# A spectral layer fused with a rational MLP on one core: padded input, later tables, ten first-stage tasks at the end of batch 0, and an offset copied into PSUM instead of added by a matmul

## The chip, the cores and the metric

The kernel runs on one core of a Trainium2 chip. The metric is device microseconds (us) of that core, median of three runs. TensorE (PE) multiplies, VectorE (DVE), ScalarE (ACT) and GpSimd (POOL) do elementwise work, SyncE (SP) issues most DMAs. [...]

## What is computed

```python
X = np.fft.rfft(x, axis=1)                       # x: 4 batches, 3008 rows, 256 columns
Yr = Xr @ w_r - Xi @ w_i + b_r
Yi = Xr @ w_i + Xi @ w_r + b_i
Y = soft_threshold(Yr, 0.01) + 1j * soft_threshold(Yi, 0.01)
x = np.fft.irfft(Y, n=3008, axis=1)              # then, row by row:
h = x @ w_in                                     # 256 -> 2048
g = (a0 + a1*h + a2*h**2 + a3*h**3) / (1 + |b0|*|h| + |b1|*h**2 + 1e-6)
out = g @ w_out                                  # 2048 -> 256
```

`w_in` and `w_out` come as 64-bit floats; the chip turns them into pairs of 32-bit numbers.

## The kernel before

A transform of length 3008 = 64 x 47 is done in two stages. For each batch, 16 first-stage tasks (`f1_task`, L158) multiply a tile of `x` by the table `f1` and put the result in HBM (`s1`). Twelve second-stage tasks (`f2_task`, L209) read it back in another order. Twelve mixing tasks (`m_task`, L237) multiply by `w_r` and `w_i`, 24 matmuls each, add the offsets `b_r`, `b_i` and threshold. Twelve `i1_task`s (L264) start the inverse transform and store to HBM (`s2`); `i2_task` (L307) ends it, two per block of five columns. The MLP then runs in 208 units (`h` L350, the rational function on ACT, DVE, POOL and an adding DMA `v<-s`, `acc` L440).

**Batch 0** runs alone, ahead of the MLP. Its first stage is a loop over 16 tasks; its tiles `a` go to HBM by SP (L187). PE then runs `warm(38)`, matmuls on zeros (L509), while the tiles come back as `b_all`. The loop at L612 makes 15 rounds, p = 0 to 14. In round p PE does `f2_task(p)`, then the two halves of `m_task(p-2)`, then `i1_task(p-3)`. ACT, DVE and POOL do what belongs to them (`x` L221, L224, L230; `yt` L258, L261; `zt` L145/L147), and between these the conversion of the weights, called by `convert(n)`, which makes n steps of `from_f64`: ACT's `e` and `r` (L482, L483), DVE's L485 and L487, DVE's L489 followed by ACT's copy `win` or `wsp` (L494), POOL's L496. The tuples `HC` and `HM` say how many steps stand ahead of `yt` and behind it in each round. An m task opens its PSUM bank `pm` with one matmul, `selr` by `bias` (L245), which writes the offsets; the 24 others (L252) add to them. `prepare_small` (L526) makes `selr` and `bias` on DVE behind the last first-stage tasks.

**Batch 0's end.** After the rounds, six more first-stage tasks of batch 1 run (two have run in round 13, eight in all, `FILL = 8`), with two conversion steps behind each; then the first two `i2_task`s and the first product `h` (unit 0).

**The main part** walks through the units i; in each, the letters of `order` say when PE products, ACT's two halves and the transform tasks of the next batch are issued. Batch 1's other first-stage tasks go into its first units. There the offsets are put into the bank by an ACT copy of the tile `offset` (L242, from unit 3 on).

Of the kernel before, what the change touches and what calls it, by code (L numbers as in the profile page):

```python
# [9 lines left out]
F32 = mybir.dt.float32  # L10
# [4 lines left out]
ALU = mybir.AluOpType  # L15
# [21 lines left out]
def dft_tables():  # L37
# [14 lines left out]
    for g in range(NG):  # L52
# [24 lines left out]
    i2p = i2b.reshape(96, TJ)  # L77
    sel = np.zeros((4, 130))
    sel[0:2, 0:64] = 1.0
    sel[2:4, 64:128] = 1.0  # L80
    sel[0::2, 128] = 1.0
    sel[1::2, 129] = 1.0
    f = np.float32
# [11 lines left out]
def spectral_moe(ctx, tc, t, out):  # L95
# [37 lines left out]
    def load_x(b, c):  # L133
        if b == 1 and c in (2, 3):
            xt = pro3.tile([96, 4, D], F32, tag=f"x{c}", name="xin", bufs=1)
        elif b == 0 and c >= 2:
            xt = const.tile([128, 4, D], F32, tag=f"win{c}", name="xin")[:96]
# [19 lines left out]

    def f1_task(b, i):  # L158
        c, r = divmod(i, 2)
        if i == 0:  # L160
            s1[b] = dram.tile([NK, NG, 2, NJ, D], F32, tag="s1", name="s1")
        pt = bank(b, "f1" if r else "")
        nc.tensor.matmul(out=pt, lhsT=f1, rhs=xin[b, c][:, 2 * r:2 * r + 2, :].rearrange("p j d -> p (j d)"),  # L163
                         start=True, stop=True)
        yield
        if b == 0:
            if not r:
                a_t[0] = const.tile([128, 4, D], F32, tag=f"wsp{c}", name="a")[:96]
            at = a_t[0][:, 2 * r:2 * r + 2]
        else:  # L170
            if early:
                at = pro.tile([128, 2, D], F32, tag="a" if i < 6 else "wt", name="a", bufs=6 if i < 6 else 2)[:96]
            else:
                at = sm.tile([128, 2, D], F32, tag="a", name="a", bufs=3)[:96]
        copy(i % 2 if early else 0, at.rearrange("p j d -> p (j d)"), pt[:96])
        yield
        if r:
            del xin[b, c]
            ahead = 4 if b == 1 and c < 4 else 2
            if b and c + ahead < NJ // 4 and not (b == 1 and c in (2, 3)):  # L180
                if early:
                    hold.append(lambda: load_x(b, c + ahead))
                else:
                    load_x(b, c + ahead)
        if b == 0:
            if r:
                nc.sync.dma_start(out=s1[b].rearrange("k g c j d -> (k g c) j d")[:, 4 * c:4 * c + 4, :], in_=a_t[0])  # L187
# [46 lines left out]
    y_t = {}  # L234
    copied = []
# [28 lines left out]
    def i1_task(b, p):  # L264
# [186 lines left out]
    def drain(g):  # L451
        for _ in g:
            pass

    def fft_tasks(b):
        ts = [(0.87, 1, 1, f1_task(b, i), 0) for i in range(16)]
        ts += [(0.0, 0, 0, load_first(b), 0)] + [(0.0, 0, 0, iter(()), 0)]
# [40 lines left out]
    with tc.manual_schedule():  # L498
        nc.vector.memset(cb, 1.0)
        nc.scalar.activation(out=cb, in_=cb, func=ACTF.Abs_reciprocal_sqrt)  # L500
        nc.sync.dma_start(out=f1, in_=t["f1"])
        b_all = [pro3.tile([128, 6, D], F32, tag=f"b{z}", name="b_all", bufs=1) for z in range(4)]
        nc.vector.memset(offset[:, 0], 0.0)
        idle = offset[:, 0].bitcast(mybir.dt.bfloat16)

# [13 lines left out]
        def load_small():
            nc.sync.dma_start(out=sel, in_=t["sel"])  # L520
            for k, nm in enumerate(("b_r", "b_i")):
                nc.sync.dma_start(out=bsb[2 * k:2 * k + 2, :],
                                  in_=t[nm].rearrange("(o d) -> o d", o=1).to_broadcast([2, D]))
            nc.sync.dma_start(out=eye, in_=t["minus"])

        def prepare_small():  # L526
            nc.vector.memset(v32(selr), 0.0)
            nc.vector.memset(v32(bias), 0.0)
            nc.vector.tensor_copy(selr[:4], sel[:, 0:128])
            nc.scalar.activation(out=minus, in_=eye, func=ACTF.Copy)  # L530
            bhi = bias[:4, 0]
            nc.vector.tensor_copy(bhi, bsb)
            nc.vector.tensor_tensor(out=blo, in0=bsb, in1=v32(bhi), op=ALU.subtract)
            nc.vector.tensor_scalar(out=bsb, in0=v32(bhi), scalar1=sel[:, 128:129], scalar2=None, op0=ALU.mult)
            for k in range(2):
                nc.vector.scalar_tensor_tensor(out=bias[:4, k], in0=blo, scalar=sel[:, 129:130], in1=bsb, op0=ALU.mult, op1=ALU.add)

# [73 lines left out]
        first = fft_tasks(1)  # L611
        for p in range(np_ + 3):  # L612
            if p < np_:
                f2g = f2_task(0, p)
                next(f2g)
                next(f2g)
# [39 lines left out]
            if p == 8:  # L656
                root()
                for k, nm in enumerate(("b_r", "b_i")):
                    for z in range(2):
                        nc.sync.dma_start(out=offset[64 * k:64 * k + 64, z],  # L660
                                          in_=t[nm].rearrange("(o d) -> o d", o=1).to_broadcast([64, D]))
# [30 lines left out]
        for i in range(-1, nu + 4):  # L692
# [111 lines left out]
```

## Time and profile before

| | us |
|---|---|
| median of 3 runs | 1453.56 (1453.04 to 1459.46) |
| the profiled execution | 1454.01 |
| its span in the trace | 1452.2 |
| PE busy | 1421.4 (98%) |
| DVE busy | 1297.3 (89%) |
| ACT busy | 1135.9 (78%) |
| POOL busy | 668.6 (46%) |

The profile is of one execution. Its own time is 1.8 us above the span and 0.45 us above the median. Times in its views count from the span's start. Matmuls overlap on PE, so a matmul's row is longer than the step to the next one. [...]

### The profile page before, as it was taken

What the parts mean: (1) busy time and instruction counts of PE and PEld (TensorE: products, weight loads), DVE (VectorE), ACT (ScalarE), POOL (GpSimd) and SP (SyncE); (2) the same over time, 40 slices, a digit from 0 to 9 for tenths busy, and PEclk for the clock granted to TensorE, in tenths of its full rate; (3) what the DMA queues carried; (4) which work ended last, traced back from release to release, by engine and by line L of the source; (5) the groups of instructions that cost most, each with busy time, mean ns of one, the idle gap of its engine ahead of it and who ended that gap; (6) DMA issues with size and microseconds to landing.
All of it is one profiled execution on the core that took longest, in us unless ns stands there. A gap on an engine that the chain in (4) does not pass through costs nothing.

```text
span 1452.2 us, 20182 instructions
## 1 busy us (share of the span) xinstructions
PE 1421.4 (98%) x7437; PEld 1242.8 (86%) x7439; DVE 1297.3 (89%) x1303; ACT 1135.9 (78%) x1438; POOL 668.6 (46%) x446
## 2 busy tenths in 40 slices
PE   8989999999999999999999999999999999999996
PEld 3966999999878999999888899998988888888886
DVE  3776889999888998898889999999989999999998
ACT  2657778787787777778888788878778988889885
POOL 0433444444444444444445445454445555555553
PEclk9998999999999999999999999999999999999999
DMA  8956545446575554554586455555455555546443
GB/s 264 374 177 154 120 104 122 104 103 134 130 189 130 124 111 103 122 131 95 121 195 149 105 118 104 121 111 119 92 114 118 107 107 108 116 98 121 92 93 70
DMA packets 84437, 187.60 MB, mean 129 GB/s; under 512 B 8363, under 2 KB 42835, under 8 KB 84339
## 3 DMA queue, kind: packets, MB, share of 16 engines
q0 software_dynamic: 30976, 98.58, 38.0%
q1 hardware_dynamic: 52467, 86.16, 18.6%
q10 hardware_dynamic: 896, 1.57, 0.3%
q8 instruction: 59, 0.97, 0.3%
q14 instruction: 39, 0.32, 0.1%
HBM read 50.23 MB, written 37.49 MB: 60 GB/s over the span
## 4 chain that ended last, share of the span: by engine, by line
PE 75%; DVE 9%; issue 8%; DMA 4%; ACT 3%; SPq 0%; ACTq 0%; DVEq 0%; POOL 0%; POOLq 0%
PE h L350 29%; PE acc L440 28%; PE pft L252 7%; PE pi L316 4%; PE pft L163 3%; DVE t L397 3%; DMA v<-s 2%; PE pft L270 2%; DVE v L408 2%; PE pft L216 2%; DVE g L406 1%; DMA raw_win<-in_w_in 1%; DVE e L489 1%; DMA s<-a 1%; DVE t L398 1%
## 5 line engine op out<-in xcount | busy, mean ns | idle before, releaser
L440 PE MATMUL acc<-g,wsp 128*128 128x470 f32 (+1 forms) x2496 | 561.2, 373 | 6.0 <-DVE g L419 6.0
L413 POOL TENSOR_TENSOR t<-t,v 128x940 f32<-128x940 f32 (+1 forms) x206 | 477.3, 2317 | 121.4 <-DVE v L408 107.8
L440 PEld LDWEIGHTS acc<-g,wsp 128*128 128x128 f32 x2496 | 466.2, 189 | 67.7 <-DVE g L419 6.9
L383 POOL DMA_DIRECT2D v<-s x208 | 186.3, 896 | 571.9 <-issue 526.7
L350 PE MATMUL h<-xsh,win 128*128 128x470 f32 (+1 forms) x1664 | 440.7, 387 | 7.1 <-DVE t L398 5.3
L350 PEld LDWEIGHTS h<-xsh,win 128*128 128x128 f32 x1664 | 305.0, 191 | 59.1 <-issue 12.7
L381 ACT ACTIVATE v<-h 128x940 f32<-128x940 f32 (+1 forms) x208 | 196.2, 943 | 155.9 <-PE h L350 155.4
L406 DVE SCALAR_TENSOR_TENSOR g<-t,small,y 128x940 fp32r<-128x940 f32 (+1 forms) x208 | 255.2, 1227 | 61.2 <-ACT y L392 59.7
L397 DVE TENSOR_TENSOR t<-t,h 128x940 f32<-128x940 f32 (+1 forms) x208 | 231.4, 1113 | 38.2 <-ACT t L385 37.7
L398 DVE SCALAR_TENSOR_TENSOR t<-t,small,h 128x940 f32<-128x940 f32 (+1 forms) x208 | 245.2, 1179 | 7.4
L419 DVE SCALAR_TENSOR_TENSOR g<-t,small,y 128x940 fp32r<-128x940 f32 (+1 forms) x208 | 244.1, 1173 | 0.1
L350 PE MATMUL h<-xsl,win 128*128 128x470 f32 (+1 forms) x832 | 243.3, 374 | 0.0
L408 DVE SCALAR_TENSOR_TENSOR v<-v,g 128x940 f32<-128x940 f32 (+1 forms) x208 | 231.7, 1114 | 0.0
L390 ACT ACTIVATE y<-v 128x940 f32<-128x940 f32 (+1 forms) x208 | 205.6, 988 | 17.2 <-DMA v<-s 17.0
L385 ACT ACTIVATE t<-h,small 128x940 f32<-128x940 f32 (+1 forms) x208 | 215.7, 1037 | 0.0
L392 ACT ACTIVATE y<-y 128x940 f32<-128x940 f32 (+1 forms) x208 | 203.7, 979 | 2.3
L382 ACT ACTIVATE s<-h 128x940 f32<-128x940 f32 (+1 forms) x208 | 195.3, 939 | 0.0
L350 PEld LDWEIGHTS h<-xsl,win 128*128 128x128 f32 x832 | 156.2, 189 | 20.9
L252 PE MATMUL pft<-wrh,x 128*128 128x256 f32 x288 | 76.6, 288 | 1.1 <-ACT pft L147 1.1
L252 PE MATMUL pft<-wih,x 128*128 128x256 f32 x288 | 75.4, 283 | 0.4 <-DVE x L228 0.4
L316 PEld LDWEIGHTS pi<-small,ct 96*128 96x128 f32 x512 | 65.1, 192 | 5.5 <-ACT a L147 3.0
L316 PE MATMUL pi<-small,ct 96*128 96x94 f32 x512 | 64.3, 272 | 2.1 <-ACT a L147 2.1
(88 smaller groups left out, 1110.5 us busy)
## 6 DMA issues: line engine op xcount, KB each, us to landing
v<-s POOLq DMA_DIRECT2D x200, 470.0 KB, 4.6
xin<-in_x SPq DMA_DIRECT2D x32, 384.0 KB, 6.6
s<-zt SPq DMA_DIRECT2D x48, 256.0 KB, 2.7
out_t<-ob SPq DMA_DIRECT2D x50, 235.0 KB, 4.5
ct<-s SPq DMA_DIRECT2D x21, 480.0 KB, 5.2
bt<-s SPq DMA_DIRECT2D x36, 256.0 KB, 3.9
s<-a SPq DMA_DIRECT2D x40, 192.0 KB, 4.2
raw_win<-in_w_in SPq DMA_DIRECT2D x8, 512.0 KB, 10.3
```

Of the source, the lines that this page charges most:

```text
L252: nc.tensor.matmul(out=pt[:, k, :], lhsT=l, rhs=r, start=False, stop=n == len(ops) - 1, skip_group_check=True)
L350: nc.tensor.matmul(out=h[:, i, :w], lhsT=l, rhs=r, start=k == 0, stop=k == len(halves) // FU - 1)
L385: nc.scalar.activation(out=d["t"], in_=h, func=ACTF.Identity, scale=rate["a3"], bias=ca[:, 2:3])
L390: nc.scalar.activation(out=d["y"], in_=d["v"], func=ACTF.Square, bias=C0)
L392: nc.scalar.activation(out=d["y"], in_=d["y"], func=ACTF.Abs_reciprocal_sqrt)
L397: nc.vector.tensor_tensor(out=tt, in0=tt, in1=h, op=ALU.mult)
L398: nc.vector.scalar_tensor_tensor(out=tt, in0=tt, scalar=ca[:, 1:2], in1=h, op0=ALU.add, op1=ALU.mult)
L406: stt(out=hi, in0=tt, scalar=ca[:, 0:1], in1=y, op0=ALU.add, op1=ALU.mult)
L408: stt(out=v, in0=v, scalar=C0, in1=v32(hi), op0=ALU.add, op1=ALU.mult)
L413: nc.gpsimd.tensor_tensor(out=tt[:, :cut], in0=tt[:, :cut], in1=v[:, :cut], op=ALU.subtract)
L419: stt(out=lo, in0=tt, scalar=ca[:, 0:1], in1=y, op0=ALU.add, op1=ALU.mult)
L440: nc.tensor.matmul(out=acc[n][e][:, :w], lhsT=l, rhs=r, start=begun[n] == 1 and seen[e] == 1, stop=begun[n] == UB and seen[e] == 3 * FU)
```

## The change

Nine things are changed.

1. `x` is laid out as one block of 128 rows by 4 KB for each tile (96 rows of data, 32 of zeros), and tiles are loaded with 128 rows; tile 0 of batch 0 in two halves. `w_r` and `w_i` are laid out so that a row is contiguous.
2. The table `f1` is loaded by ACT's queue, `f2`, `w_r`, `w_i` behind all first-stage stores, `eye` behind `f2`. The last first-stage tile is stored in two halves.
3. `sel`, `bsb`, `selr`, `bias` and `prepare_small` are gone. The tile `offset` is loaded by four DMAs between the fourth and the fifth tile of `x`.
4. The matmul L245 is gone. `m_begin` copies `offset` into the bank by ACT. For batch 0 it is called at the head of rounds 2 to 13, ahead of `f2_task`.
5. `minus` is made in round 8 behind `root`.
6. All twelve copies `zt` of batch 0 are made by DVE (six by ACT before).
7. `warm(38)` becomes `warm(23)`, `warm(7)` becomes `warm(8)`.
8. `FILL` goes from 8 to 10, with one conversion step per task instead of two; `HM` is 6 instead of 4 in rounds 12 and 13. Tasks 12 and 13 of batch 1 run ahead of 8 to 11.
9. In units 0 to 3 `order` puts ACT's first-stage copies (`e`) ahead of the second half of the function (`Y`, `y`).

```diff
-WARM = 38
-FILL = 8
+WARM = 23
+FILL = 10
-HM = (0, 0, 3, 3, 3, 3, 3, 3, 3, 3, 3, 3, 4, 4)
+HM = (0, 0, 3, 3, 3, 3, 3, 3, 3, 3, 3, 3, 6, 6)
...
-            xt = sm.tile([96, 4, D], F32, tag="xin", name="xin")
-        nc.sync.dma_start(out=xt, in_=t["x"][b, :, 4 * c:4 * c + 4, :])
-        xin[b, c] = xt
+            xt = sm.tile([128, 4, D], F32, tag="xin", name="xin")
+        for r in (0, 2) if b + c == 0 else (0,):
+            w = 2 if b + c == 0 else 4
+            nc.sync.dma_start(out=xt[:, r:r + w], in_=t["x"][b, c, :, r:r + w, :])
+        xin[b, c] = xt[:96]
...
+    def m_begin(b):
+        m_t[b] = bank(b, "m").rearrange("p (k d) -> p k d", k=2)
+        copy(0, m_t[b], offset)
+
     def m_task(b, p, k):
-        if k == 0:
-            m_t[b] = bank(b, "m").rearrange("p (k d) -> p k d", k=2)
+        if k == 0 and b:
+            m_begin(b)
         pt = m_t[b]
         xs = x_t[b, p]
-        if k == 0 and copied:
-            copy(0, pt, offset)
-        elif k == 0:
-            nc.tensor.matmul(out=pt, lhsT=selr, rhs=bias, start=True, stop=False, skip_group_check=True)
...
-        copy(b == 0 and p % 2 == 0, zt.rearrange("p k d -> p (k d)"), pt.rearrange("p k d -> p (k d)"))
+        copy(b == 0, zt.rearrange("p k d -> p (k d)"), pt.rearrange("p k d -> p (k d)"))
...
-        load_small()
         for i in range(16):
-            drain(f1_task(0, i))
-            if i == 9:
-                load_f2(0, 4)
-                load_wt()
-            if i == 13:
-                prepare_small()
-            if i == 15:
-                prepare_mix()
+            drain(f1_task(0, i, i))
+        load_f2(0, 4)
+        load_wt()
+        prepare_mix()
...
         for p in range(np_ + 3):
+            if 2 <= p < np_ + 2:
+                m_begin(0)
             if p < np_:
                 f2g = f2_task(0, p)
...
         for _ in range(FILL - 2):
             drain(first.pop(0)[3])
-            convert(2)
+            convert(1)
...
-            order = "F1AasYehmy2" if storing(i) else "Fs1AaYehmy2"
+            order = "Fs1AaehmYy2" if i < 4 else "F1AasYehmy2" if storing(i) else "Fs1AaYehmy2"
```

**ACT in rounds 2 to 4.** First the program before, from the threshold `yt` of round 2 to the one of round 4 (a `yt` reads the bank `pm` that the round's m task has filled; `x` is ACT's half of the round's second-stage tile):

```order
L258 ACTIVATE yt_347<-pm_321 128x512
L482 ACTIVATE e_350<-raw_win1_221 128x512
L483 ACTIVATE r_351<-raw_win1_221 128x512
L494 ACTIVATE win0_355<-e_315 128x2x256
L221 ACTIVATE x_365<-pft_360 128x4x128
L482 ACTIVATE e_374<-raw_win2_275 128x512
L483 ACTIVATE r_375<-raw_win2_275 128x512
L258 ACTIVATE yt_404<-pm_378 128x512
L494 ACTIVATE win1_408<-e_350 128x2x256
L221 ACTIVATE x_425<-pft_420 128x4x128
```

The same stretch of the changed program, whose lines have other numbers (L252 is `yt`, L477 and L478 are `e` and `r`, L489 is `win`, L217 is `x`, L144 the copy of the offsets):

```order
L252 ACTIVATE yt_324<-pm_277 128x512
L477 ACTIVATE e_327<-raw_win1_213 128x512
L478 ACTIVATE r_328<-raw_win1_213 128x512
L489 ACTIVATE win0_332<-e_294 128x2x256
L144 ACTIVATE pm_337<-offset_73 128x512
L217 ACTIVATE x_344<-pft_339 128x4x128
L477 ACTIVATE e_353<-raw_win2_252 128x512
L478 ACTIVATE r_354<-raw_win2_252 128x512
L252 ACTIVATE yt_381<-pm_337 128x512
L489 ACTIVATE win1_385<-e_327 128x2x256
L144 ACTIVATE pm_397<-offset_73 128x512
L217 ACTIVATE x_404<-pft_399 128x4x128
```

The copy into `pm` stands behind the conversion's last step of the round before (`win`) and ahead of `x`. PE's first matmul of the m task that writes this `pm` waits for ACT.

**SP at the program's start.** Before (`s` is HBM behind the first stage, `a` its tiles, `f` the table `f2`):

```order
L501 DMA small<-in_f 96x128
L140 DMA xin<-in_x 96x1024 x8
L520 DMA sel<-in_sel 4x130
L522 DMA bsb<-in_b_r 2x256
L522 DMA bsb<-in_b_i 2x256
L524 DMA eye<-in_minus 128x128
L187 DMA s_131<-a 96x1024 x5
L579 DMA f_70<-in_f 128x512
L589 DMA wt<-in_w_r 128x2x256
L589 DMA wt<-in_w_i 128x2x256
L187 DMA s_131<-a 96x1024 x3
L576 DMA b_all<-s_131 128x2x256 x3
```

And in the changed program:

```order
L137 DMA xin<-in_x 128x512 x2
L137 DMA xin<-in_x 128x1024 x3
L509 DMA offset<-in_b_r 64x256 x2
L509 DMA offset<-in_b_i 64x256 x2
L137 DMA xin<-in_x 128x1024 x4
L183 DMA s_129<-a 96x1024 x7
L183 DMA s_129<-a 96x512 x2
L561 DMA f_70<-in_f 128x512
L571 DMA wt<-in_w_r 128x512
L571 DMA wt<-in_w_i 128x512
L558 DMA b_all<-s_129 128x2x256 x2
```

The eight stores now follow one another with no table between them, and four loads of `offset` stand between the tiles of `x`.

**ACT in unit 1.** Before (`v`, `s`, `t` are the first half of the function for unit 1, `y` the second half for unit 0, which reads `v` behind the adding DMA, `a` two copies of first-stage tiles):

```order
L381 ACTIVATE v_1161<-h_1113 128x940
L382 ACTIVATE s_1160<-h_1113 128x940
L385 ACTIVATE t_1162<-h_1113,small_69 128x940
L390 ACTIVATE y_1167<-v_1127 128x940
L147 ACTIVATE a_1169<-pft_1143 96x512
L147 ACTIVATE a_1171<-pft_1145 96x512
L392 ACTIVATE y_1167<-y_1167 128x940
```

And changed:

```order
L375 ACTIVATE v_1147<-h_1101 128x940
L376 ACTIVATE s_1146<-h_1101 128x940
L379 ACTIVATE t_1148<-h_1101,small_69 128x940
L144 ACTIVATE a_1153<-pft_1129 96x512
L144 ACTIVATE a_1155<-pft_1131 96x512
L384 ACTIVATE y_1157<-v_1115 128x940
L386 ACTIVATE y_1157<-y_1157 128x940
```

The two copies `a` have moved ahead of the `y` that waits for the adding DMA.

## Rows read from the trace of the kernel before

**Rows 1.** Windows by stage: busy time, then PEclk, DMA share and GB/s.

```profile
0.00:36.05 36.05, 29.88 (x108) 14.15 (x110) 11.07 (x22) 8.87 (x15) 1.43 (x6) 1.00 0.88 263
36.05:93.53 57.48, 56.09 (x420) 53.49 (x419) 42.73 (x71) 36.88 (x68) 23.62 (x22) 1.00 0.85 296
93.53:108.21 14.68, 10.91 (x40) 5.59 (x38) 10.32 (x16) 8.52 (x16) 4.40 (x4) 0.96 0.68 212
108.21:146.55 38.34, 35.55 (x130) 26.78 (x131) 24.99 (x24) 28.30 (x36) 13.02 (x10) 0.84 0.65 155
146.55:1300.00 1153.45, 1150.86 (x6023) 1021.44 (x6021) 1061.48 (x1023) 934.59 (x1153) 549.03 (x352) 1.00 0.56 120
```

**Rows 2.** Timeline of PE from the start: start, length, what, wait before it.

```profile
5.18 13.97 PE L163 MATMUL pft<-xin,small 96*128 96x512 f32 x32 [0.78 <-DMA xin<-in_x]
...
30.21 1.13 PE L216 MATMUL pft<-f,b_all 128*128 128x128 f32 x8 [2.86 <-issue]
...
35.16 1.13 PE L216 MATMUL pft<-f,b_all 128*128 128x128 f32 x8 [1.21 <-DMA f<-in_f]
```

**Rows 3.** The chain that ended last, pieces in order of time.

```profile
21.55 5.80 DMA s<-a
...
140.44 5.09 DMA bt<-s
```

**Rows 4.** Windows: loads of 96 rows alone, and of 128 rows mostly.

```profile
6.00:15.00 9.00, 9.00 (x22) 3.97 (x21) 3.44 (x5) 3.07 (x6) 0.00 (x0) 1.00 1.04 247
32.00:60.00 28.00, 26.74 (x204) 25.37 (x205) 17.80 (x29) 16.41 (x30) 10.41 (x11) 1.00 1.05 377
```

**Rows 5.** DMA issues on the page: form, count, KB each, median us to landing.

```profile
s<-a SPq DMA_DIRECT2D x8, 384.0 KB, 5.0
s<-a ACTq DMA_DIRECT2D x8, 192.0 KB, 2.4
```

**Rows 6.** The removed matmul by its line: count, ns min/median/max, first and last start.

```profile
L245 PE MATMUL pm<-bias,selr x12: 475/478/582, 36.0 to 90.1; 128*128 128x512 f32 x12
```

**Rows 7.** Timeline of PE, one round: offset matmul, first and last of 24, next round's.

```profile
44.90 0.48 PE L245 MATMUL pm<-bias,selr 128*128 128x512 f32 x1
45.21 0.28 PE L252 MATMUL pm<-wrh,x 128*128 128x256 f32 x1
...
47.97 0.28 PE L252 MATMUL pm<-wih,x 128*128 128x256 f32 x1
...
49.76 0.48 PE L245 MATMUL pm<-bias,selr 128*128 128x512 f32 x1
```

**Rows 8.** Timeline of ACT, rounds 3 and 4, and round 6.

```profile
44.12 0.58 ACT L258 ACTIVATE yt<-pm 128x512 f32<-128x512 f32 x1
46.12 0.63 ACT L494 ACTIVATE win<-e 128x512 fp32r<-128x512 f32 x1 [1.42 <-DVE e L489]
46.65 0.58 ACT L221 ACTIVATE x<-pft 128x512 fp32r<-128x512 f32 x1
...
59.23 0.58 ACT L258 ACTIVATE yt<-pm 128x512 f32<-128x512 f32 x1
59.71 0.67 ACT L482 ACTIVATE e<-raw_win 128x512 f32<-128x512 f32 x1
...
62.07 0.63 ACT L494 ACTIVATE win<-e 128x512 fp32r<-128x512 f32 x1 [1.13 <-DVE e L489]
```

**Rows 9.** Timeline of ACT: unit 0's wait, and an offset copy of batch 1.

```profile
123.08 0.99 ACT L390 ACTIVATE y<-v 128x940 f32<-128x940 f32 x1 [2.37 <-DMA v<-s]
...
157.59 0.60 ACT L147 ACTIVATE pft<-offset 128x512 f32<-128x512 f32 x1 [2.14 <-DVE xsl L327]
```

**Rows 10.** Timeline of PE: unit 0, the third first-stage pair, the first `acc`.

```profile
108.21 3.50 PE L350 MATMUL h<-xsh,win 128*128 128x470 f32 x8 [1.22 <-ACT xsh L319]
...
124.60 3.78 PE L163 MATMUL pft<-xin,small 96*128 96x512 f32 x4 [2.39 <-ACT a L147]
...
136.31 2.74 PE L440 MATMUL acc<-g,wsp 128*128 128x470 f32 x12
```

More of the change, by code (lines that the diff above doesn't have):

```diff
@@ L77, in dft_tables @@
     i2p = i2b.reshape(96, TJ)
[L78 to L82, printed above, removed]
     f = np.float32
@@ L134, in load_x @@
         if b == 1 and c in (2, 3):
-            xt = pro3.tile([96, 4, D], F32, tag=f"x{c}", name="xin", bufs=1)
+            xt = pro3.tile([128, 4, D], F32, tag=f"x{c}", name="xin", bufs=1)
+        elif b == 1 and c >= 6:
+            xt = sm.tile([128, 6, D], F32, tag="x", name="xin", bufs=2)[:, :4]
         elif b == 0 and c >= 2:
-            xt = const.tile([128, 4, D], F32, tag=f"win{c}", name="xin")[:96]
+            xt = const.tile([128, 4, D], F32, tag=f"win{c}", name="xin")
         else:
-            xt = sm.tile([96, 4, D], F32, tag="xin", name="xin")
-        nc.sync.dma_start(out=xt, in_=t["x"][b, :, 4 * c:4 * c + 4, :])
-        xin[b, c] = xt
+            xt = sm.tile([128, 4, D], F32, tag="xin", name="xin")
[3 more added lines that the diff above has]
+        xin[b, c] = xt[:96]
     def copy(eng, out, in_):
@@ L178, in f1_task @@
             del xin[b, c]
[L179 to L184, printed above, removed]
+            if b == 1 and c < 2:
+                hold.append(lambda: load_x(b, c + 4))
+            elif b > 1 and c + 2 < NJ // 4:
+                load_x(b, c + 2)
         if b == 0:
-            if r:
-                nc.sync.dma_start(out=s1[b].rearrange("k g c j d -> (k g c) j d")[:, 4 * c:4 * c + 4, :], in_=a_t[0])
+            z = slice(2 * r, 2 * r + 2) if i >= 14 else slice(0, 4)
+            if r or i >= 14:
+                nc.sync.dma_start(out=s1[b].rearrange("k g c j d -> (k g c) j d")[:, 4 * c + z.start:4 * c + z.stop, :], in_=a_t[0][:, z])
             return
@@ L455, in fft_tasks @@
     def fft_tasks(b):
-        ts = [(0.87, 1, 1, f1_task(b, i), 0) for i in range(16)]
+        turns = [*range(8), *range(12, 16), *range(8, 12)] if b == 1 else range(16)
+        ts = [(0.87, 1, 1, f1_task(b, i, pos), 0) for pos, i in enumerate(turns)]
         ts += [(0.0, 0, 0, load_first(b), 0)] + [(0.0, 0, 0, iter(()), 0)]
@@ L499, in spectral_moe @@
         nc.vector.memset(cb, 1.0)
+        nc.scalar.dma_start(out=f1, in_=t["f1"])
         nc.scalar.activation(out=cb, in_=cb, func=ACTF.Abs_reciprocal_sqrt)
-        nc.sync.dma_start(out=f1, in_=t["f1"])
         b_all = [pro3.tile([128, 6, D], F32, tag=f"b{z}", name="b_all", bufs=1) for z in range(4)]
-        nc.vector.memset(offset[:, 0], 0.0)
-        idle = offset[:, 0].bitcast(mybir.dt.bfloat16)
+        nc.vector.memset(blank, 0.0)
+        idle = blank.bitcast(mybir.dt.bfloat16)
         def warm(n, kind=""):
@@ L509, in warm, with load_offset @@
                 nc.tensor.matmul(out=pt, lhsT=idle[:, :128], rhs=idle, start=True, stop=True)
-        warm(7)
-        for c in range(8):
+        def load_offset():
+            for k, nm in enumerate(("b_r", "b_i")):
+                for z in range(2):
+                    nc.sync.dma_start(out=offset[64 * k:64 * k + 64, z],
+                                      in_=t[nm].rearrange("(o d) -> o d", o=1).to_broadcast([64, D]))
+        warm(8)
+        for c in range(4):
             load_x(0, c)
-        sel = pro.tile([4, 130], F32, tag="sel", name="sel", bufs=1)
-        bsb = pro.tile([4, D], F32, tag="bsb", name="bsb", bufs=1)
-        blo = pro.tile([4, D], F32, tag="blo", name="blo", bufs=1)
+        load_offset()
+        for c in range(4, 8):
+            load_x(0, c)
         eye = pro.tile([128, 128], F32, tag="eye", name="eye", bufs=1)
[L519 to L536, printed above, removed]
         def prepare_mix():
@@ L657, in spectral_moe @@
                 root()
[L658 to L661, printed above, removed]
+                nc.scalar.activation(out=minus, in_=eye, func=ACTF.Copy)
         load_rates()
@@ L787 @@
     x = np.asarray(inputs["x"])
-    xp = np.zeros((B, NG, ROWS, NJ, D), x.dtype)
-    xp[:, :, :N2] = x.reshape(B, N2, NG, NJ, D).transpose(0, 2, 1, 3, 4)
-    arrays = {"x": xp.reshape(B, NG * ROWS, NJ, D), **dft_tables()}
+    xp = np.zeros((B, NJ // 4, 128, 4, D), x.dtype)
+    for g in range(NG):
+        xp[:, :, g * ROWS:g * ROWS + N2] = x.reshape(B, N2, NG, NJ // 4, 4, D)[:, :, g].swapaxes(1, 2)
+    arrays = {"x": xp, **dft_tables()}
     for k, n in (("w_r", "w_r"), ("w_i", "w_i"), ("b_r", "b_r"), ("b_i", "b_i"),
```

25 lines of the change are left out of this document (12 added, 13 removed).

## Prediction

> **What bounds the kernel now.** I read the windows by stage first. From 146.55 us on PE is busy for all but 2.6 of 1153.45 us [rows 1], and the change leaves that work alone, but for two first-stage tasks that go to batch 0's end and the order in units 0 to 3. What it can win or lose lies ahead of 146.55, in four stages: the first stage up to 36.05, the rounds up to 93.53 (PE busy 56.09 of 57.48), batch 0's end up to 108.21 (10.91 of 14.68), and the first units up to 146.55 (35.55 of 38.34, at a mean granted clock of 0.84) [rows 1]. Since PE is the bound behind them, a microsecond won or lost there is one at the end. Then I read the timeline of PE and the chain for each stage: PE's tasks end at 5.18 + 13.97 = 19.15, but the last store lands only at 21.55 + 5.80 = 27.35, the next stage begins at 30.21 and round 2 at 35.16, behind a wait of 1.21 for the table `f2` [rows 2, 3].
>
> **First stage.** The tiles come in at 247 GB/s while 96 rows are loaded, against 377 GB/s in a stretch that loads mostly 128 rows [rows 4]. A tile of 384 KB takes 1.59 us by the one, one of 512 KB takes 1.39 us by the other, and PE needs 13.97/16 = 0.87 us a task, 1.75 a tile [rows 2]: either way the load keeps ahead, so padding buys at most the 0.78 us that PE waits at the start [rows 2]. The gain lies behind it. `prepare_small` no longer delays the last copy, no table goes ahead of the last store, and this store is half as long. PE ends by about 18.6; a copy later (0.7, like the other ACT and DVE rows of this size, 0.58 to 0.60 [rows 8, 9]) the last half is issued, at 19.3. The same 192 KB from ACT's queue land after 2.4 us, 384 KB behind other stores after 5.0 [rows 5]: 21.7 to 24.3, in place of 27.35. I take 22.8, as seven stores still stand in the queue. That is 4.5 earlier (3.0 to 5.7). The wait of 1.21 for `f2` goes too, since the table comes in halves. **First stage: -5.7, from -3 to -7.** The shorter warm-up, 23 matmuls instead of 38, fills the shorter wait and costs nothing unless the wait stays long.
>
> [...]
>
> **The rounds: what goes.** The offset matmul takes 45.21 - 44.90 = 0.31 us of PE's time in each of 12 rounds [rows 6, 7]. A round is 49.76 - 44.90 = 4.86 long [rows 7], so PE alone would come to 4.55.
>
> **The rounds: what comes.** The copy that replaces it takes 0.60 [rows 9], and ACT would have the time. But it stands at the head of ACT's round, behind the conversion's last step of the round before, and PE's m task waits for it. Rows of before show where ACT is at this place, just ahead of `x`: in round 4 it comes to `x` at 46.65, while PE began the m task at 45.21 [rows 7, 8]. In before that costs nothing, since PE uses `x` two rounds later. Now it is a cycle: PE ends the 24 matmuls, ACT starts `yt`, DVE finishes `yt`, then DVE's conversion step (L489), then ACT's `win`, then the copy, then PE. The links, from the rows: the 24 matmuls 47.97 + 0.28 - 45.21 = 3.04 [rows 7]; `yt` to `win` 46.12 - 44.12 = 2.00, with 1.42 of it waiting for DVE, or 62.07 - 59.23 = 2.84 where another DVE step stands between; `win` to the next instruction 0.53; `yt` to the next 0.48 [rows 8]; the copy 0.60 [rows 9]; about 0.05 for each of two semaphores, my estimate. From the order of the changed program each round has one of four lengths:
>
> - 3.04 + 0.1 + 2.00 + 0.53 + 0.60 = 6.27, where `win` stands behind `yt`: rounds 2, 3, 7, 8.
> - 7.11 with 2.84 for 2.00: rounds 6, 11, 12.
> - 3.04 + 0.1 + 0.48 + 2 x 0.53 + 0.60 = 5.28, where only `e` and `r` stand there: rounds 5, 10.
> - 4.55, PE's own, where nothing does: rounds 4, 9.
>
> Together 25.1 + 21.3 + 10.6 + 9.1 = 66.1 us from the first m task to the twelfth, against 90.1 - 36.0 = 54.1 [rows 6]: +12.0. In round 8 the steps of `root` and the copy `minus` stand ahead of the copy too, behind DVE; by the nearest wait of that kind I add 1.4. **Rounds: +13.4, from +9** (if ACT and DVE, which now have time to spare, answer faster than in before) **to +15.** The lower end of all, the copy hidden, is 11 x 0.31 = -3.4, a rival below. The six `zt` that go to DVE, 0.6 each, lie in rounds that are now longer than DVE's work (42.73 busy of 57.48 [rows 1]), hence 0; in rounds of 4.55 they would fill DVE. The padded and earlier DMAs are hidden by the same slack.
>
> **Clock.** PE now waits 1.7 to 2.6 us in seven of the rounds. [...] The stretch at 0.84 lost 0.16 x 38.34 = 6.1 us of PE's work in two falls. In the rounds, where PE is not busy all the time, I take one fall at 2.5. **Clock: +2.5, from 0 to +10.**
>
> **Batch 0's end.** Two more first-stage tasks are 1.75 us of PE, in a stage where PE is idle for 14.68 - 10.91 = 3.8 [rows 1]; conversion steps go from 12 to 8 there. ACT, which paces it (unit 0 begins behind ACT's `xsh` [rows 10]), has one more copy, two more DMA issues and four fewer steps. **0, from -2 to +2;** without the idle time +1.75.
>
> **First units.** Now ACT stands 2.37 us at unit 0's `y` for the adding DMA with two first-stage copies behind it [rows 9], and PE waits 2.39 for these [rows 10]. The copies now go first: that wait goes, the fourth pair of tasks is gone (1.75), and if the second clock fall stays away, 3.1 more: 7.2 in all. What is late next: unit 2's `h` products still need ACT's first half, which still stands behind the adding DMA; and the second stage of batch 1 now comes one unit earlier, while its load, 5.09 [rows 3], still follows the last store. I take about half. **-4, from -1 to -7.**
>
> **Sum.** -5.7 + 13.4 + 2.5 + 0 - 4 = +6.2 on the profiled execution's 1454.0: 1460.2, and 0.45 less against the median: 1460.
>
> **Rivals.**
> *The copy does not hold PE* (the other side). If ACT reaches the copy within the 1.5 us of other PE work between two m tasks, the rounds give -3.4 instead of +13.4, no clock fall: -5.7 - 3.4 - 4 = -13, 1441. For it: rounds 4 and 9 do just this; against it: 46.65 against 45.21, and a semaphore that PE must wait for. It decides at a `yt` to `win` time of about 0.3 us. 13%.
> *The clock falls in most of the long rounds:* three or four falls at 2.5 to 3.1 instead of one, +7: 1467. [...] 17%. [...]
> *The first units give all 7, and the first fall at unit 0 stays away as well,* as more tasks stand ahead of it: 4 to 6 more, 1455. 15%.
>
> **Numbers.** My forecast (1460, its own range 1454 to 1467) has 55%. A change under 0.5%, 7.3 us, can hardly be told from none here, so "same" is 1446 to 1461. The forecast splits evenly between same and slower; the clock rival is slower; the first-units rival is same but for 0.02; the hidden copy is faster. Faster 0.15, same 0.42, slower 0.43. The range leaves out the hidden copy and the far end of the clock: 1447 to 1470.
>
> **What would show it.** Right: in the changed profile PE waits for ACT's copy ahead of the m tasks, about 1.5 to 2.5 us in seven rounds, and first to twelfth m task take 63 to 69 us; round 2's m task begins near 30.5 instead of 36.4; the wait of PE for ACT's first-stage copies in unit 2 is gone. Wrong: rounds of 4.6 to 4.9 us, a first stage that waits for tiles, or a granted clock of 1.00 all through (then 1457) or below 0.9 in the rounds (then 1467).

## The result, and the profile after

The changed kernel takes 1472.19 us in the median of 4 runs (1470.34 to 1473.60), the kernel before 1454.50 beside it: a ratio of 1.0115, 95% interval 1.0099 to 1.0132. It is slower, by more than the forecast of 1460 and outside its range of 1447 to 1470. The profiled execution took 1470.34 with a span of 1468.6, 16.4 more than before's.

The windows of the changed kernel by the same stages as in [rows 1] (first stage, rounds, batch 0's end, first units, the rest); the number behind the five engines is the granted clock, 1.00 being full speed:

```profile
0.00:35.90 35.90, 30.13 (x96) 14.42 (x96) 8.60 (x14) 9.17 (x15) 0.94 (x6) 0.95 0.92 315
35.90:112.77 76.87, 59.17 (x408) 55.48 (x407) 45.43 (x78) 41.73 (x76) 24.48 (x24) 0.93 0.66 233
112.77:128.10 15.33, 12.82 (x45) 6.50 (x45) 9.53 (x16) 8.10 (x15) 3.44 (x3) 1.00 0.62 203
128.10:163.40 35.30, 30.64 (x134) 24.32 (x135) 26.78 (x26) 29.14 (x36) 13.72 (x11) 0.95 0.69 157
163.40:1300.00 1136.60, 1133.37 (x5937) 1007.00 (x5935) 1042.92 (x1005) 917.23 (x1132) 538.66 (x345) 1.00 0.56 121
```

The whole loss lies in the second row, 76.87 in place of 57.48 us, with 17.7 of PE idle and a mean granted clock of 0.93. The first row has hardly moved.

| stage | forecast | measured |
|---|---|---|
| first stage | -5.7 | 35.90 - 36.05 = -0.15 |
| rounds, and the clock in them | +13.4 and +2.5 | 76.87 - 57.48 = +19.4, of which about 5.1 is clock, 14.3 the rest |
| batch 0's end | 0 | 15.33 - 14.68 = +0.65 |
| first units | -4 | 35.30 - 0.84 - 38.34 = -3.9 |
| rest | 0 | +0.4 |

(The first units now hold one second-stage task more, 0.84. The 5.1 is an estimate from the three windows below that lie in the rounds: 0.43 x 4.00 + 0.50 x 3.30 + 0.30 x 5.70.) The sum is +16.4, as the spans have it.

**The rounds.** The waits of PE from 36 to 113 us (us in total, times, longest), ACT's timeline at the place of [rows 8], and PE's m task behind it:

```profile
PE pm L246 <- ACT pm L144: 17.1, 9, 3.1
```

```profile
45.52 0.60 ACT L252 ACTIVATE yt<-pm 128x512 f32<-128x512 f32 x1 [1.64 <-PE pm L246]
47.47 0.63 ACT L489 ACTIVATE win<-e 128x512 fp32r<-128x512 f32 x1 [1.36 <-DVE e L484]
48.01 0.58 ACT L144 ACTIVATE pm<-offset 128x512 f32<-128x512 f32 x1
48.53 0.58 ACT L217 ACTIVATE x<-pft 128x512 fp32r<-128x512 f32 x1
```

```profile
48.65 0.38 PE L246 MATMUL pm<-wrh,x 128*128 128x256 f32 x1 [1.47 <-ACT pm L144]
```

`yt` to `win` takes 1.95, as in [rows 8]; then comes the copy, in the order listed for the program, and PE starts 0.06 behind its end (0.05 was the estimate for a semaphore). Nine of the twelve copies hold PE. From one m task to the next:

| round | 2 | 3 | 4 | 5 | 6 | 7 | 8 | 9 | 10 | 11 | 12 |
|---|---|---|---|---|---|---|---|---|---|---|---|
| forecast | 6.27 | 6.27 | 4.55 | 5.28 | 7.11 | 6.27 | 7.67 | 4.55 | 5.28 | 7.11 | 7.11 |
| changed kernel | 6.39 | 6.36 | 4.64 | 5.78 | 7.39 | 6.37 | 7.72 | 6.17 | 5.52 | 7.08 | 8.97 |
| copy ahead, zt shared (below) | 3.77 | 4.63 | 4.63 | 4.63 | 5.25 | 5.86 | 4.63 | 4.64 | 6.60 | 3.64 | 6.34 |

Nine of eleven lie within 0.5 of the forecast; rounds 9 and 12 have a clock fall within.

**The clock.** Windows of the changed kernel around its four falls up to the first units:

```profile
30.00:34.50 4.50, 4.50 (x22) 3.39 (x23) 1.10 (x2) 0.73 (x2) 0.61 (x1) 0.62 1.05 343
81.90:85.90 4.00, 4.00 (x19) 3.78 (x19) 0.96 (x2) 1.87 (x4) 1.28 (x1) 0.57 0.25 92
99.30:102.60 3.30, 3.28 (x15) 3.28 (x16) 0.02 (x1) 0.00 (x0) 1.47 (x2) 0.50 0.26 84
109.30:115.00 5.70, 5.70 (x25) 4.61 (x25) 1.34 (x3) 1.74 (x3) 0.00 (x0) 0.70 0.52 151
```

Each comes behind a wait of PE: 3.72, 2.83, 3.08 and 1.80 us. Three lie in the rounds, where the forecast had one; they cost about 1.7 us each, where it had 2.5. Waits of 2.39 and 2.50 in the same execution brought none, so the length of the wait alone does not tell them apart.

**The first stage.** PE's timeline, and the chain of the same time:

```profile
4.62 3.08 PE L160 MATMUL pft<-xin,small 96*128 96x512 f32 x4
7.95 5.54 PE L160 MATMUL pft<-xin,small 96*128 96x512 f32 x12 [0.26 <-DMA xin<-in_x]
14.05 7.11 PE L160 MATMUL pft<-xin,small 96*128 96x512 f32 x16 [0.56 <-DMA xin<-in_x]
...
29.84 1.13 PE L212 MATMUL pft<-f,b_all 128*128 128x128 f32 x8 [3.72 <-DMA b_all<-s]
```

```profile
21.91 3.73 DMA s<-a
...
25.73 4.03 DMA b_all<-s
```

PE starts 0.56 earlier than before but ends at 14.05 + 7.11 = 21.16, not at 18.6: it waits for the tiles behind the loads of `offset`. The last store then lands 3.73 after its issue, as forecast (3.5), at 25.64; the load of `b_all` takes 4.03, where 30.21 - 27.44 = 2.8 from SP's issue to the second stage had been taken over from before. From the second stage's start to the first m task it is 35.90 - 29.84 = 6.06 at a low clock, where 6.15 - 1.21 = 4.9 follows from the rows of before.

### The profile page after: what moved, and what is told of

It is laid out like the page before. It is cut to its first block, busy times and chain, and to the rows that moved or that the text cites. A ratio compares the mean times of both kernels' runs of the same rounds, so it can differ in the third digit from the quotient of the medians.

```text
span 1468.6 us, 20148 instructions
## 1 busy us (share of the span) xinstructions
PE 1420.8 (97%) x7413; PEld 1243.3 (85%) x7413; DVE 1296.2 (88%) x1302; ACT 1139.5 (78%) x1443; POOL 667.9 (45%) x446
## 4 chain that ended last, share of the span: by engine, by line
PE 76%; DVE 8%; issue 7%; DMA 5%; ACT 3%; SPq 0%; ACTq 0%; POOL 0%; DVEq 0%; POOLq 0%
PE h L344 28%; PE acc L434 28%; PE pft L246 7%; PE pi L310 4%; PE pft L160 3%; DVE t L391 2%; DVE v L402 2%; PE pft L212 2%; PE pft L264 2%; DMA v<-s 2%; PE pm L246 2%; DMA s<-a 1%; DVE g L400 1%; DMA xin<-in_x 1%; DVE t L392 1%
## 5 line engine op out<-in xcount | busy, mean ns | idle before, releaser
L384 ACT ACTIVATE y<-v 128x940 f32<-128x940 f32 (+1 forms) x208 | 205.6, 989 | 14.3 <-DMA v<-s 14.3
L160 PE MATMUL pft<-xin,small 96*128 96x512 f32 x128 | 62.0, 607 | 3.1 <-ACT a L144 2.0
```

Source lines behind the costliest of these rows:

```text
L384: nc.scalar.activation(out=d["y"], in_=d["v"], func=ACTF.Square, bias=C0)
```

## The experiments

Theory: ACT's copy stands behind the conversion step, so PE waits for it; it is the place that costs, not the copy. The first stage's gain was lost to the loads of `offset` between the tiles and to the clock. Rivals: DVE, which got all the `zt`, makes the rounds long; the padded bytes make the first stage long. Times are medians with the ratio to the kernel before, run beside it. First and twelfth m task and the first `h` are from the timelines of PE, in one profiled execution each; four kernels with one and the same first stage (the changed one, x2, x5, x8) have their first m task between 35.9 and 37.6, so 1 us there tells little. The granted clock differs among them: in the window of 30 to 36 us it is 0.72 in the changed kernel and 0.54 in x5; from 20 to 36 us it is 0.89 in x8 and 0.79 in x5, from 28 to 37 us 0.62 in x2.

| | first m | twelfth m | apart | first h | median | ratio |
|---|---|---|---|---|---|---|
| before | 36.36 | 90.47 | 54.1 | 108.21 | | |
| changed | 35.90 | 108.29 | 72.4 | 128.10 | 1472.19 | 1.0115 (1.0099 to 1.0132) |
| x1 | 36.61 | 112.34 | 75.7 | 130.23 | 1476.58 | 1.0147 (1.0119 to 1.0175) |
| x2 | 37.02 | 93.68 | 56.7 | 112.88 | 1457.81 | 1.0008 (0.9991 to 1.0025) |
| x3 | 33.51 | 111.41 | 77.9 | 131.62 | 1469.27 | 1.0096 (1.0074 to 1.0118) |
| x4 | 33.76 | 108.76 | 75.0 | 128.91 | 1473.30 | 1.0126 (1.0096 to 1.0157) |
| x5 | 37.58 | 92.20 | 54.6 | 110.49 | 1452.62 | 0.9991 (0.9981 to 1.0001) |
| x6 | 36.67 | 91.28 | 54.6 | 109.59 | 1453.44 | 0.9990 (0.9979 to 1.0001) |
| x7 | 40.58 | 95.20 | 54.6 | 113.08 | 1460.36 | 1.0044 (1.0032 to 1.0056) |
| x8 | 36.33 | 92.99 | 56.7 | 111.40 | 1455.83 | 1.0010 (1.0000 to 1.0021) |
| x9 | 33.55 | 90.72 | 57.2 | 109.45 | 1452.10 | 0.9987 (0.9970 to 1.0004) |
| x10 | 36.27 | 91.71 | 55.4 | 110.07 | 1453.28 | 0.9991 (0.9976 to 1.0006) |
| x11 | 35.78 | 90.38 | 54.6 | 108.42 | 1450.20 | 0.9972 (0.9957 to 0.9987) |
| x12 | 32.45 | 89.74 | 57.3 | 108.08 | 1452.05 | 0.9990 (0.9979 to 1.0001) |

### x1: the kernel before, with the copy alone

```diff
-            nc.tensor.matmul(out=pt, lhsT=selr, rhs=bias, start=True, stop=False, ...)
...
         for p in range(np_ + 3):
+            if 2 <= p < np_ + 2:
+                m_t[0] = bank(0, "m").rearrange("p (k d) -> p k d", k=2)
+                copy(0, m_t[0], offset)
```

The four loads of `offset`, in round 8 before, go ahead of the raw weights for this.

> The kernel before, with one part of the change alone: for batch 0 the offsets are copied into the bank by ACT at the head of rounds 2 to 13, and the matmul that added them is gone (two DVE operations of the start that only served it are gone too, and the offsets are loaded behind the first-stage loads). Theory (the copy stands on ACT behind the conversion step and PE's m task waits for it): the first m task still begins near 36, the first to the twelfth takes 68 to 73 us in place of 54.1, and the time is 1468 to 1473. Rival (the long rounds come from the six zt copies that went to DVE, or from the other moved work): 52 to 58 us from the first to the twelfth, and a time of 1451 to 1458.

The copy alone makes the kernel slower than the whole change does: 75.7 us from the first to the twelfth m task, more than the theory's 73, and far from the rival's 58. The time is above the expected 1473 too. The mean granted clock from 36 to 115 us is 0.94. Waits of PE from 36 to 116, and ACT's timeline:

```profile
PE pm L250 <- ACT pm L147: 20.0, 11, 5.7
```

```profile
35.96 0.60 ACT L147 ACTIVATE pm<-offset 128x512 f32<-128x512 f32 x1 [2.49 <-DMA offset<-in_b_i]
...
42.03 0.66 ACT L480 ACTIVATE e<-raw_win 128x512 f32<-128x512 f32 x1 [4.96 <-DMA raw_win<-in_w_in]
```

The last row shows something that the theory did not have. ACT's first conversion step waits for the first raw weights, here until 42.03 since the loads of `offset` go ahead of them; the next copy stands behind it on ACT, and PE waits 5.7 for that. In the kernel before ACT waited there too, and no one on PE felt it:

```profile
38.61 0.68 ACT L482 ACTIVATE e<-raw_win 128x512 f32<-128x512 f32 x1 [1.68 <-DMA raw_win<-in_w_in]
```

### x2: the changed kernel, with the copy one round ahead

```diff
-            if 2 <= p < np_ + 2:
-                m_begin(0)
             if p < np_:
                 f2g = f2_task(0, p)
                 next(f2g)
                 next(f2g)
             if p < 2:
                 warm(4, "m")
+            if 1 <= p < np_ + 1:
+                m_begin(0, p - 1)
```

> The changed kernel, with ACT's copy for round p+1 issued in round p, behind x, in the bank that is free by then; nothing else differs. Theory (only the place of the copy makes PE wait): PE no longer waits for the copy, the first to the twelfth m task takes 50 to 55 us in place of 72.4, the granted clock stays at 1.00 in the rounds, and the time is 1450 to 1456. Rival (the rounds are bound by DVE, which has all zt copies, or by ACT's added 0.6 us a round): 60 us or more, and a time of 1460 or more.

PE does not wait for the copy once. 15.7 of the 18.3 us that the twelfth m task had lost against the first come back, the granted clock is 1.00 from 37 to 98 us, and the time is no longer told apart from before's. The 56.7 us and the median lie a little above what the theory had, and well below the rival. The place of the copy was the cost, with the falls of the clock that its waits brought. What is left in the rounds are other waits of PE, from 37 to 97:

```profile
PE pft L264 <- DVE x L220: 2.8, 2, 2.0
PE pft L264 <- DVE zt L142: 2.3, 3, 1.7
PE pft L264 <- DVE yt L255: 0.7, 1, 0.7
```

So the rival has a small part: once the copy is out of the way, DVE with all its `zt` holds PE for 2.3 us.

### x3: the loads of the offsets behind the tables

```diff
-        load_offset()
         for c in range(4, 8):
             load_x(0, c)
...
         nc.sync.dma_start(out=eye, in_=t["minus"])
+        load_offset()
```

> The changed kernel, with the four loads of the offsets moved from between the fourth and the fifth tile to behind all tables of the first stage. Theory (these loads, not the padded rows, keep PE waiting for the fifth tile): PE's sixteenth first-stage task ends near 19.4 in place of 21.2, the last store lands near 24, the second stage begins near 28 in place of 29.8, and the time is 1.5 to 2 us below the changed kernel's. Rival (the padded tiles bring more bytes, and the load is late for that): the sixteenth task ends at 20.8 or later, and the time does not move.

The sixteenth first-stage task ends at 19.56, the second stage begins at 27.73, the first m task at 33.51, 2.4 earlier than in the changed kernel: the loads between the tiles were one part of the missing gain. PE's first-stage tasks now follow one another without a wait, here and in x9 below, which moves the loads too:

```profile
4.62 14.94 PE L160 MATMUL pft<-xin,small 96*128 96x512 f32 x32
```

```profile
4.61 14.25 PE L160 MATMUL pft<-xin,small 96*128 96x512 f32 x32
```

The 0.7 between them lies at the start: the first three matmuls take 1.06, 1.06 and 0.78 us in x3, and 0.79, 0.59 and 0.59 in x9. The windows of 4 to 6 us show a granted clock of 1.00 in both, so what lengthened them was not shown. In the changed kernel the first three are as slow; but x5, where they take 0.70, 0.59 and 0.59, ends its sixteenth task at 21.15 all the same, since PE waits longer for the tiles there.

But rounds 2 and 3 now take 8.31 and 8.71, and by the twelfth m task the gain is gone. ACT and PE in round 2:

```profile
37.51 0.66 ACT L477 ACTIVATE e<-raw_win 128x512 f32<-128x512 f32 x1 [3.12 <-DMA raw_win<-in_w_in]
```

```profile
41.82 0.58 PE L246 MATMUL pm<-wrh,x 128*128 128x256 f32 x1 [4.30 <-ACT pm L144]
```

The raw weights land near 37 whether the rounds begin earlier or not (here the moved loads of `offset` go ahead of them; in x4, where they don't, ACT's wait ends at 36.99), and the longer wait of PE costs clock as well: the first matmul behind it takes 0.58, where it took 0.38 in the changed kernel, and the mean granted clock from 36 to 100 us is 0.89. The median is 2.9 below the changed kernel's, with intervals that overlap; the profiled execution is 1.7 longer. This doesn't decide the 1.5 to 2 us that were expected.

### x4: 38 warm-up matmuls

```diff
-WARM = 23
+WARM = 38
```

> The changed kernel, with 38 warm-up matmuls behind the first stage in place of 23. Theory (the 3.72 us that PE waits for the loads behind the shorter warm-up lets the clock fall, which then costs the start of the rounds): PE waits under 1 us, the granted clock is 1.00 from 30 to 36 us, the second stage still begins near 29.8, the first m task near 34.4 in place of 35.9, and the time is 1 to 2 us below the changed kernel's. Rival (the clock falls whatever the warm-up, or the tables set the first m task): the first m task stays within 0.5 of 35.9.

PE no longer waits ahead of the second stage, and the window of 30 to 36 us shows a granted clock of 1.00, where the changed kernel has 0.62 from 30 to 34.5:

```profile
30.00:36.00 6.00, 5.92 (x45) 4.81 (x44) 1.38 (x2) 2.29 (x4) 1.23 (x2) 1.00 1.02 323
```

From the second stage to the first m task it is 33.76 - 29.05 = 4.71 in place of 6.06. So the shorter warm-up cost 1.35 us at this place, against "costs nothing". Again rounds 2 and 3 (7.56 and 7.85) take it back behind the raw weights, and the time is no less.

### x5: the copy ahead, and zt shared

```diff
-        copy(b == 0, zt.rearrange(...), ...)
+        copy(b == 0 and p % 2 == 0, zt.rearrange(...), ...)
```

> The changed kernel with the copy one round ahead, and the copies zt shared as before: six by DVE, six by ACT. Theory (with the copy ahead, what is left of the long rounds are PE's waits for DVE's zt and x, which the all-DVE zt brings): the first to the twelfth m task takes 51 to 54.5 us in place of 56.7, and the time is 2 to 4 us below that with zt all on DVE, 1452 to 1456. Rival (ACT, which now has the offset copy and half of zt, takes DVE's place as the late one): 56 us or more, the same time or longer.

54.6 us, just above the theory's 54.5; the waits for DVE's `zt` are gone, one of 1.0 for ACT's `zt` has come. The time is within the expected range, but not told apart from x2's: the intervals of the ratios overlap. Giving all `zt` to DVE cost some 2 us of the rounds, hidden in the changed kernel behind the waits for the copy.

### x6: the offsets by ACT's queue, and 38 warm-up matmuls

```diff
-                    nc.sync.dma_start(out=offset...
+                    nc.scalar.dma_start(out=offset...
...
+        load_offset()
         load_f2(0, 4)
         load_wt()
```

(and, as in x5, the copy ahead and `zt` shared, with `WARM = 38`)

> The changed kernel with the copy one round ahead, zt shared, the four loads of the offsets issued by ACT's queue behind the first stage, and 38 warm-up matmuls. Theory (with the copy ahead a shorter first stage is no longer eaten by the wait of ACT for the first raw weights): the first m task begins between 32 and 34.5, the twelfth 51 to 55 us later, the granted clock stays at 1.00 up to 90 us, and the time is 1446 to 1451. Rival (the first raw weights, which land near 37, hold the rounds whichever engine comes first): the second to the fourth round are longer by what the first m task is earlier, and the time is that of the kernel with the copy ahead and zt shared.

A miss: the first m task begins at 36.67, not at 32 to 34.5. The four issues take ACT from 19.52 to 22.29, SP issues the tables later (`f2` at 24.09, in the changed kernel at 22.90), and PE waits 2.08 for ACT's copy of `w_i`. The time is that of x5.

### x7: the kernel before, with the copy ahead

As x1, with the copy one round ahead and the offsets loaded by ACT's queue behind the last first-stage copy.

> The kernel before, with the offsets copied by ACT one round ahead, in place of the matmul, and loaded by ACT's queue behind the first stage; zt, first stage and order as before. Theory (the copy itself is cheaper than the matmul, 0.31 us of PE a round, and costs only where it stands): the rounds take 50.5 to 54 us from the first to the twelfth m task, and the time is 1450 to 1454, the same or just below before. Rival (copies on ACT lengthen the rounds wherever they stand): 56 us or more, 1457 or more.

The rounds take 54.6, hardly more than with the matmul (54.1) and just above the theory's 54. The copy in its right place costs next to nothing and gains nothing: rounds that PE bounds are 4.63 in place of 4.86, but four of eleven are bounded by DVE or ACT. The time, outside the theory's 1454, is longer for another reason, which SP's own waits and PE's timeline show:

```profile
SPq L585 <- DMA offset<-in_b_r: 4.5, 2, 4.3
```

```profile
34.39 2.05 PE L216 MATMUL pft<-f,b_all 128*128 128x128 f32 x8 [6.75 <-issue]
```

SP's load of `w_r` waited 4.3 us for a load that ACT had issued, and the last three stores stood behind it.

### x8: the copy ahead, with batch 0's end and the units as before

```diff
-FILL = 10
+FILL = 8
-            convert(1)
+            convert(2)
-            order = "Fs1AaehmYy2" if i < 4 else "F1AasYehmy2" ...
+            order = "F1AasYehmy2" ...
```

(and `HM` with 4, 4 at its end)

> The changed kernel with the copy one round ahead, and batch 0's end and the order of units 0 to 3 as before: six first-stage tasks there with two conversion steps behind each, and ACT's first-stage copies behind the second half of the function. Theory (the ten tasks and the order gain about 4 us from the first h to the first second-stage task of batch 1, and lose about 2 at batch 0's end): 1 to 4 us slower than the kernel with the copy ahead alone. Rival (they gain nothing, or lose): the same time or less.

The median is 2.0 below x2's, with overlapping intervals: the theory did not come out, and the ten tasks and the new order gained nothing that can be told. The 3.9 us that the first units gained in the changed kernel are real in its profile, but part of this is two tasks that were done earlier (1.75).

### x9: both repairs of the first stage, without a copy that holds PE

x5, with the move of x3 and `WARM = 36`.

> The kernel with the copy one round ahead and zt shared, and also the loads of the offsets behind the first stage's tables and 36 warm-up matmuls: both repairs of the first stage at once, with no copy that holds PE. Theory (the earlier start is worth something only until ACT's first conversion step, which waits for raw weights that land near 37): the first m task begins at 31 to 33.5 in place of 37.6, the second to the fourth round are longer by some of it, the twelfth begins at 88 to 91 in place of 92.2, and the time is 1449 to 1452. Rival (all of it is passed on): the twelfth begins at 86 to 88, and the time is 1446 to 1449. Second rival (none of it is): 1452 or more.

The first theory holds in kind: of 4.0 us at the first m task 1.5 are left at the twelfth, and the time is at the edge of its 1452. Rounds 3 and 4 take 5.66 and 5.73 in place of 4.63. ACT's wait for the raw weights, and PE's waits from the first m task on:

```profile
38.17 0.67 ACT L477 ACTIVATE e<-raw_win 128x512 f32<-128x512 f32 x1 [3.67 <-DMA raw_win<-in_w_in]
```

```profile
33.55 0.39 PE L246 MATMUL pm<-wrh,x 128*128 128x256 f32 x1 [0.65 <-ACT pm L144]
...
40.95 1.10 PE L264 MATMUL pft<-yt,g 128*128 128x256 f32 x4 [0.51 <-DMA g<-in_g]
...
46.96 1.10 PE L264 MATMUL pft<-yt,g 128*128 128x256 f32 x4 [0.84 <-DVE x L220]
```

DVE's `x` of round 4 stands behind conversion steps, which run late. But the raw weights are not the only arrival in the way: PE also meets the load of the table `g`, and the first m task itself waits for the copy, since ACT waits until 32.90 for the moved loads of `offset` (1.39 in x12).

### x10: the tables between the stores

```diff
         for i in range(16):
             drain(f1_task(0, i, i))
-        load_f2(0, 4)
-        load_wt()
+            if i == 9:
+                load_f2(0, 4)
+                load_wt()
```

(on x5)

> The kernel with the copy one round ahead and zt shared, and the tables f2, w_r and w_i loaded between the stores, behind the tenth first-stage task, as in the kernel before. By the prediction's step (no table ahead of the last store, so that it lands earlier): the second stage begins 1 us or more later than at 30.97. Rival (behind the stores the tables share the DMA engines with the loads of b_all, 4.03 us in place of 2.8, so that moving them gained nothing): the second stage begins within 1 us of 30.97 or earlier, and the time is the same.

The second stage begins at 30.46, half a us earlier than in x5 and within the 29.84 to 30.97 of the four kernels with one first stage. SP issues the first load of `b_all` at 27.66, not at 26.36, and from there to the second stage it is 2.8 in place of 4.6: what the last store gained, the load behind it lost. The rival was right; moving the tables was worth nothing.

### x11: 96 rows of each tile

```diff
-            nc.sync.dma_start(out=xt[:, r:r + w], in_=t["x"][b, c, :, r:r + w, :])
+            nc.sync.dma_start(out=xt[:96, r:r + w], in_=t["x"][b, c, :96, r:r + w, :])
```

(on x5)

> The kernel with the copy one round ahead and zt shared, with the same padded layout in HBM, but only the 96 rows of data loaded, 384 KB a tile in place of 512. [...] If the bytes count (the 377 GB/s that the sum used, with 33% more bytes): the sixteenth task ends 1 us or more earlier, and the first m task too.

The sixteenth task ends at 20.34, 0.8 earlier than in x5, where 1 us or more was expected if the bytes count. The second stage begins 2.4 earlier, and this is the fastest kernel of all, 0.9972 (0.9957 to 0.9987) of before, 4.1 us. Its interval lies clear of 1, so it beats both kernels. Whether the 96 rows did it isn't settled: x12 has them too.

### x12: all of it

> All repairs at once: the copy one round ahead, zt shared, the loads of the offsets behind the first stage's tables, 36 warm-up matmuls, and only 96 rows of each tile loaded. Theory (an earlier start is given back in the second to the fourth round, where ACT waits for raw weights): the first m task begins at 31 to 33.5, the twelfth at 88.5 to 90.7, the time is 1449 to 1451, that of the kernel with 96 rows or a little less. Rival (the two gains of the first stage add up in full, 4.0 and 1.8 at the first m task): the twelfth begins at 86.5 to 88, and the time is 1446 to 1448.

The first m task at 32.45, the twelfth at 89.74, as the theory says; the gains don't add up. The time is above the expected 1451 and no better than x5's. With the loads of `offset` out of the way the sixteenth task ends at 18.90 with 96 rows and at 18.86 with 128 (x9). The windows of 8 to 14 us, x9 and then x12:

```profile
8.00:14.00 6.00, 6.00 (x15) 2.59 (x15) 2.31 (x4) 1.96 (x4) 0.00 (x0) 1.00 1.01 401
```

```profile
8.00:14.00 6.00, 6.00 (x15) 2.65 (x14) 2.28 (x4) 2.14 (x4) 0.00 (x0) 1.00 1.04 249
```

At the same busy share of the DMA engines they move 401 and 249 GB/s: an estimated 1.31 us for a tile of 512 KB and 1.58 for one of 384 KB (some stores lie in both stretches). Both are ahead of PE's 1.75 a tile, so padding could not gain anything here, as the prediction said.

## Why the prediction was wrong

**The copy: right, in mechanism and size.** About 14.3 us without the clock against 13.4, with the forecast lengths round by round. From the first to the twelfth m task it is 72.4 and not 63 to 69, as two falls of the clock lie within. x2 shows that it is the place: same copy, one round earlier, and the waits are gone. The six `zt` at 0: right while the copy holds PE; 2.1 us once it doesn't (56.7 in x2, 54.6 in x5).

**The step that failed: "First stage: -5.7".** It gave -0.15 in the changed kernel, and "a first stage that waits for tiles", one of the prediction's own signs of being wrong, came true. Three links of its sum were off.
- "PE ends by about 18.6": 21.16. The term looked at the tiles' own bytes, and not at the four loads put between them. x3 gives 1.6 us of it back by moving these alone (19.56), and in x9, which moves them too, the sixteenth task ends at 18.86.
- "`b_all`" behind the store, taken over from before at about 2.8: 4.03, as the tables now land beside it. x10 shows the exchange.
- The wait of 1.21 for `f2` did go, but the shorter warm-up, which "costs nothing unless the wait stays long", left a wait of 3.72 and then a granted clock of 0.62: x4 gets 1.35 back.

Behind that lay a bound which the prediction didn't name, and its premise that "a microsecond won or lost there is one at the end" fell with it. An earlier start of the rounds meets the raw weights, which land near 37: x3 and x4 begin 2.4 and 2.1 earlier and have lost it by the twelfth m task, x9 keeps 1.5 of 4.0. The row of before at 38.61 had shown this wait; it cost nothing there and was due next. The load of `g` and the moved loads of `offset` have a part of it in x9.

**The clock: right in kind, too small.** About 5.1 us in the rounds and not 2.5: three falls of 1.7 in place of one of 2.5. The rival "the clock falls in most of the long rounds", which stood at 17% and 1467, had the number of falls right and their price too high. Windows at 0.57, 0.50 and 0.70 stand behind waits of 2.83, 3.08 and 1.80, but the waits of 2.39 and 2.50 brought no fall: from 36 to 81.9 us the granted clock is 1.00.

**Batch 0's end and the first units:** +0.65 and -3.9 against 0 and -4, both in their ranges; x8 can't tell their sum from nothing. PE's wait for ACT's first-stage copies in unit 2 is gone, as forecast. Yet -3.9 beside -4 is partly luck. By the windows the clock gave about 0.16 x 38.34 - 0.05 x 35.30 = 4.4 and the tasks done earlier 1.75, while PE's idle time rose from 2.79 to 4.66. Of what the prediction named as late next, the load for batch 1's second stage did hold PE; the other wait is DVE's. PE's timeline of the changed kernel:

```profile
146.38 1.43 PE L344 MATMUL h<-xsh,win 128*128 128x470 f32 x4 [2.60 <-DVE t L392]
...
155.37 1.13 PE L212 MATMUL pft<-f,bt 128*128 128x128 f32 x8 [2.06 <-DMA bt<-s]
```

**The rival that the copy does not hold PE** was rightly set low, but its price was wrong as well: -3.4 in the rounds assumed that PE bounds each of them. With the copy out of the way they take 54.6, not 50.7 (x5, x6, x7), since DVE and ACT bound four.

Together: 5.5 of the 10.2 us that the profiled execution misses the forecast by are the first stage, about 2.6 the clock and 0.9 the waits in the rounds. That the padded rows cost nothing was right where no other load stands between the tiles: the sixteenth task ends at 18.86 in x9 and 18.90 in x12. With the loads of `offset` between them 96 rows end 0.8 earlier (x11 beside x5). x9 beside x12 shows the full tile no slower, with an estimated 1.31 us for it and 1.58 for the other.

Left open: why x11 is faster than x5 and x12, when x12 adds parts to it that gain in the profile; the intervals of the three ratios overlap.

## What to carry to other kernels

When a matmul's operand moves to another engine, ask what stands ahead of the new instruction there, not what it costs: the same 0.6 us copy cost about 14 us behind a conversion step and next to nothing one round earlier, where a free bank allowed it. A stage that starts earlier is worth what the next arrival lets through; look in the trace of before for waits that cost nothing yet. And look at what stands behind a small load on its queue: here four of 64 KB between the tiles held the first stage by 1.6 us.

## What was not expected of the hardware

Four loads of 64 KB, each of 64 rows of 1 KB, cost the first stage 1.6 us (its sixteenth task ends at 21.16 in the changed kernel, at 19.56 in x3), where 256 KB would take an estimated 0.70 at the 375 GB/s of the window before. In the window of 8 to 10 us the changed kernel moves 207 GB/s at a share of 0.72, where it moves 375 in the two before and 326 in the two behind:

```profile
6.00:8.00 2.00, 1.74 (x4) 0.42 (x2) 0.27 (x1) 0.59 (x1) 0.00 (x0) 1.00 0.95 375
8.00:10.00 2.00, 2.00 (x5) 0.81 (x6) 0.47 (x2) 0.59 (x1) 0.00 (x0) 1.00 0.72 207
10.00:12.00 2.00, 2.00 (x5) 0.84 (x5) 0.82 (x2) 0.59 (x1) 0.00 (x0) 1.00 0.96 326
```

x3, without them, moves 416 there. And putting a load on another engine's queue did not take it out of the way: in x7 SP waited 4.3 us for ACT's.
